# Adding 1e-6 to three of four attention denominators on ScalarE instead of TensorE, and moving their reciprocals

## The chip, the cores and the metric

The kernel runs on one core of one Trainium2 chip. A core has a matrix engine (TensorE, PE in the profile; its weight loads are listed apart as PEld), three engines for elementwise work (VectorE or DVE, ScalarE or ACT, GpSimd or POOL), SyncE (SP), whose queue issues most of the DMA transfers, an on-chip memory of 128 partitions (SBUF), and the accumulator memory PSUM that TensorE writes and VectorE and ScalarE read. The metric is the device time of the whole program in microseconds; lower is better.

## The reference, cut to what matters

The input x is 2048 tokens of 576 features in bfloat16. Four layers run in the order A, B, A, B, each on a layer norm of x and each added to x. A is linear attention with 32 heads of 18 features, B an MLP 576 -> 4608 -> 576 with a norm of its own in front. The same weights serve both A layers and both B layers.

```python
def _A_ref(x, wqkv, wo):
    q, k, v = qkv[0], qkv[1], qkv[2]            # of (x @ wqkv), 32 heads of 18
    phi = lambda t: jnp.where(t > 0, t + 1, jnp.exp(t)) + 1e-6
    pq, pk = phi(q), phi(k)
    kv = jnp.einsum("bhsd,bhse->bhde", pk, v)
    z = jnp.einsum("bhsd->bhd", pk)
    num = jnp.einsum("bhqd,bhde->bhqe", pq, kv)
    den = jnp.einsum("bhqd,bhd->bhq", pq, z)[..., None] + 1e-6
    o = num / den
    return (o, heads joined) @ wo

def _B_ref(x, w1, b1, w2, b2):
    y = _layernorm(x, axis=-1)
    h = _gelu(jnp.einsum("bsd,df->bsf", y, w1) + b1)
    return jnp.einsum("bsf,fd->bsd", h, w2) + b2

x = x + _A_ref(_layernorm(x, axis=-1), A_wqkv, A_wo)
x = x + _B_ref(_layernorm(x, axis=-1), B_w1, B_b1, B_w2, B_b2)
x = x + _A_ref(_layernorm(x, axis=-1), A_wqkv, A_wo)
x = x + _B_ref(_layernorm(x, axis=-1), B_w1, B_b1, B_w2, B_b2)
```

The change concerns `den`: the sum over a head's features of pq times z, plus 1e-6, and the reciprocal of it that scales the numerator.

## The kernel before, in words

All weights and x stay in SBUF. Tokens are worked on in 16 tiles of 128 and in 4 blocks of 512, numbered 0 to 3 in the code (the title of the change counts them 1 to 4). The order on every engine is the order in the source: the class InOrder (line 45) ties each instruction of VectorE (`vec`), ScalarE (`act`), GpSimd (`pool`) and SyncE (`sp`) to the one before it on that engine, and `pe` (line 217) does the same for TensorE. All matmuls go through `mm` (line 223), so they carry line 224 in the profile, and most work of the other engines carries line 53.

An A layer first walks the token tiles for keys and values, then forms the matrix of each head and multiplies it into `wo` (kv_wo). Query features pq of the four blocks are made by q_proj: TensorE projects, ScalarE evicts the result twice out of PSUM, as Exp and as Relu, and a later step `finish` on VectorE joins the two. Features are kept in five groups of up to seven heads (G = 5) with tokens along the free dimension, in slots of the tile `units`.

The denominators of a block come from den_stage (line 661). For each of five feature groups, four matmuls of 128 tokens each, in four column tiles of 32 rows, multiply pq with `zsel` (the sums of the keys, put in the columns of their heads); a sixth row of four multiplies `eps_sel`, filled with 1e-6, with the identity and so adds the 1e-6. VectorE takes the reciprocal out of PSUM into `rden`. For block 0 it is spread over the features by matmuls (scale_first). For blocks 1 to 3 it is written to DRAM (rden_rows), and `spread` (line 677) reads it back in seven transfers into `yT`, repeated for each feature of a head; scale_stage on VectorE then multiplies it into pq, and wo_stage multiplies the scaled pq with the head products and adds x (`residual`, on VectorE). wo_stage takes the bank pairs accA and accB of PSUM by turns, and so do the MLP groups.

The first MLP block is interleaved with the end of the A layer. After block 0's outputs come den_stage(1) and spread(1), a dummy Gelu that brings in the table of the Gelu (warm_table, line 782), the remaining `finish` steps, the scales of block 1, three MLP groups, den_stage(2) and (3), both spreads, the outputs of block 1, the scales of blocks 2 and 3, three more groups, the outputs of blocks 2 and 3, and two more groups. MLP groups are numbered here from 0.

An MLP group (m1_group, line 822) makes four tiles of 128 hidden features for 512 tokens. Its matmuls use half of the array's rows each, in pairs, and run in two halves of nine pairs. Between the halves, matmuls wait for a relay, a tiny copy on ScalarE (lines 864 and 865), that follows the end of other matmuls of the group. ScalarE evicts the four tiles with the Gelu and the bias b1: tiles 0 and 2 from a bank pair (hp_ps in the profile), tiles 1 and 3 from single banks (h_ps). Eviction 3 is held back until flush. Four single banks are used by turns for h_ps and den_ps.

Of the kernel before, what the change touches and what calls it, by code (L numbers as in the profile page):

```python
# [7 lines left out]
ACT = mybir.ActivationFunctionType  # L8
ALU = mybir.AluOpType
BF16 = mybir.dt.bfloat16  # L10
F32 = mybir.dt.float32
# [3 lines left out]
S, D, F, H, DH = 2048, 576, 4608, 32, 18  # L15
P = 128
# [4 lines left out]
G = 5  # L21
# [6 lines left out]
TPC = CB // P  # L28
CA = 512
# [6 lines left out]
def build(tc, A_x, A_wqkv, A_wo, B_w1, B_b1, B_w2, B_b2, out, n_layers=4):  # L36
    nc = tc.nc
    with ExitStack() as ctx:
        const = ctx.enter_context(tc.tile_pool(name="const", bufs=1))
# [52 lines left out]
        ident = const.tile([P, P], BF16, name="ident")  # L92
# [14 lines left out]
        quad_mask = const.tile([P, 4, P], BF16, name="quad_mask")  # L107
        zsel = const.tile([P, 6, H], BF16, name="zsel")
        eps_sel = const.tile([P, H], BF16, name="eps_sel")
        last_two = const.tile([P, 2], F32, name="last_two")  # L110
        zk = const.tile([P, P], BF16, name="zk")

        def mask_batches():
            sel, fill = pool.affine_select, pool.memset
            hb = head_bc[:, 0:4 * P].rearrange("p (g c) -> p g c", g=4)
            fours = head_bc[:, 4 * P:4 * P + 54].rearrange("p (h d) -> p h d", h=3)

            def maskz_a():
                first = fill(maskz[:], 1.0)
                sel(out=maskz[:], in_=maskz[:], compare_op=ALU.is_ge, fill=0.0,  # L120
                    base=0, pattern=[[-DH, 7], [0, DH]], channel_multiplier=1)
                sel(out=maskz[:], in_=maskz[:], compare_op=ALU.is_ge, fill=0.0,
                    base=DH - 1, pattern=[[DH, 7], [0, DH]], channel_multiplier=-1)
                return first

            def maskz_b():
                first = fill(zsel[:], 0.0)
                fill(eps_sel[:], 1e-6)
                fill(zk[:], 0.0)
                fill(last_two[:], 0.0)  # L130
                sel(out=last_two[:], in_=last_two[:], compare_op=ALU.not_equal, fill=1.0,
                    base=-126, pattern=[[-1, 2]], channel_multiplier=1)
                return first

            def heads_a():
                first = fill(head_sel[:], 1.0)
                part = head_sel[:, 0:5, :]
                sel(out=part, in_=part, compare_op=ALU.is_ge, fill=0.0,
                    base=0, pattern=[[126, 5], [-DH, H]], channel_multiplier=1)
                sel(out=part, in_=part, compare_op=ALU.is_ge, fill=0.0,  # L140
                    base=DH - 1, pattern=[[-126, 5], [DH, H]], channel_multiplier=-1)
                return first

            def heads_b():
                part = head_sel[:, 5, :]
                first = sel(out=part, in_=part, compare_op=ALU.is_ge, fill=0.0,
                            base=V4 - 64, pattern=[[-DH, H]], channel_multiplier=1)
                sel(out=part, in_=part, compare_op=ALU.is_ge, fill=0.0,
                    base=DH - 1 - (V4 - 64), pattern=[[DH, H]], channel_multiplier=-1)
                sel(out=part, in_=part, compare_op=ALU.is_ge, fill=0.0,  # L150
                    base=-64, pattern=[[0, H]], channel_multiplier=1)
                part = head_sel[:, 4, :]
                sel(out=part, in_=part, compare_op=ALU.is_ge, fill=0.0,
                    base=63, pattern=[[0, H]], channel_multiplier=-1)
                return first

            def quads_a():
                first = fill(quad_mask[:], 1.0)
                sel(out=quad_mask[:], in_=quad_mask[:], compare_op=ALU.is_ge, fill=0.0,
                    base=0, pattern=[[-32, 4], [0, P]], channel_multiplier=1)  # L160
                return first

            def quads_b():
                first = sel(out=quad_mask[:], in_=quad_mask[:], compare_op=ALU.is_ge, fill=0.0,
                            base=31, pattern=[[32, 4], [0, P]], channel_multiplier=-1)
                fill(head_bc[:], 0.0)
                return first

            def spread(quad):
                def ops():  # L170
                    first = sel(out=hb[:, :, 0:126].rearrange("p g (h d) -> p g h d", h=7),
                                in_=hb[:, :, 0:126].rearrange("p g (h d) -> p g h d", h=7), compare_op=ALU.not_equal, fill=1.0,
                                base=-32 * quad, pattern=[[-7, 4], [-1, 7], [0, DH]], channel_multiplier=1)
                    sel(out=fours, in_=fours, compare_op=ALU.not_equal, fill=1.0,
                        base=-32 * quad - 28, pattern=[[-1, 3], [0, DH]], channel_multiplier=1)
                    for part, n in ((hb[:, :, 126:128], [[0, 4], [0, 2]]), (head_bc[:, 4 * P + 54:4 * P + 64], [[0, 10]])):
                        sel(out=part, in_=part, compare_op=ALU.not_equal, fill=1.0,
                            base=-32 * quad - 31, pattern=n, channel_multiplier=1)
                    return first
                return ops  # L180

            return [maskz_a, maskz_b, heads_a, heads_b, quads_a, quads_b] + [spread(quad) for quad in range(4)]
# [40 lines left out]
        def mm(out_, lhsT, rhs, start, stop, **kw):  # L223
            return pe(nc.tensor.matmul(out_, lhsT=lhsT, rhs=rhs, start=start, stop=stop, **kw))  # L224
# [242 lines left out]
        def layer_A(li, next_kind, begin, before_tile, before_keys, mid_tile, rows_ahead, after_tile, q_tiles, placed, mlp):  # L467
# [192 lines left out]

            def den_stage(c):
                dp = one("den_ps", "one3" if c == 0 else None)
                for g in range(G + 1):
                    for j in range(TPC):
                        sel, by = (zsel[:, g + (g == 4 and c % 2), :], pq[(g, c)][:, j * P:(j + 1) * P]) if g < G else (eps_sel[:], ident[:])
                        mm(dp[32 * j:32 * (j + 1), 0:P], sel, by, g == 0, g == G)
                rden = work.tile([P, P], BF16, name="rden", bufs=2)
                with nc.allow_low_precision("reciprocal of the denominator in the reference's bfloat16"):
                    vec.reciprocal(out=rden[:], in_=dp[:, 0:P])
                if c > 0:  # L670

                    sp.dma_start(out=rden_rows[c].rearrange("h (j n) -> j h n", j=TPC), in_=rden[:])
                    return
                vec.tensor_tensor(out=quad_rden.rearrange("p (j n) -> p j n", j=4), in0=quad_mask[:],
                                  in1=rden[:].unsqueeze(1).to_broadcast([P, 4, P]), op=ALU.mult)

            def spread(c):
                heads, to = rden_rows[c], spare(c)
                at = 64 * (c % 2)
                for g in range(4):  # L680
                    sp.dma_start(out=to[0:126, g, :], in_=heads[7 * g:7 * g + 7, :].unsqueeze(1).to_broadcast([7, DH, CA]))
                sp.dma_start(out=to[126:P, 0:4, :], in_=heads[31:32, :].unsqueeze(1).to_broadcast([2, 4, CA]))
                sp.dma_start(out=to[at:at + 54, 4, :], in_=heads[28:31, :].unsqueeze(1).to_broadcast([3, DH, CA]))
                sp.dma_start(out=to[at + 54:at + 64, 4, :], in_=heads[31:32, :].to_broadcast([10, CA]))

            def scale_stage(g, c):
                rows = q_rows(g, c)
# [59 lines left out]
            q_next(True, "one0")  # L747
            finish(len(q_late) - 3)
            den_stage(0)
            kv_wo(0, act)  # L750
            kv_wo(1, act)
            q_next(True, "one1")
# [25 lines left out]
            q_next(True)  # L778
            first[3].transposed()
            den_stage(1)  # L780
            spread(1)
            warm_table(ACT.Gelu_apprx_tanh)
            assert not q_left
# [3 lines left out]
                for g in range(G):  # L787
                    scale_stage(g, c)

            def groups(n):  # L790
                for _ in range(n):
                    mlp.m1_group(0, mlp.done)
                    mlp.flush()

            def outputs(c):
                for t in range(c * TPC, (c + 1) * TPC):
                    wo_stage(t)

            finish(len(q_late))
            scales(1)  # L800
            groups(3)
            den_stage(2)
            den_stage(3)
            spread(2)
            spread(3)
            outputs(1)
            scales(2)
            scales(3)
            groups(3)
# [7 lines left out]
        class LayerB:  # L817
# [1 line left out]
                self.li, self.next_kind = li, next_kind  # L819
                self.hT, self.held, self.done = {}, None, 0  # L820

            def m1_group(self, c, g):
                hT = self.hT.setdefault(c, {})
                ctok = slice(c * CB, (c + 1) * CB)

# [32 lines left out]
                for i, (hi, n, wt, mv) in enumerate(order):  # L858
# [11 lines left out]
                    if n in (0, 2) and seen[0] == seen[2] == 9:  # L870
                        evict(0)
                        evict(2)
                    if n == 1 and seen[1] == 9:
                        evict(1)
                self.held = lambda: evict(3)
                self.done += 1

            def flush(self):
# [208 lines left out]
```

## Time and profile before

| | |
|---|---|
| median of 3 runs | 751.48 us (751.39 to 751.73) |
| the profiled execution | 751.55 us, its span 749.8 us |
| instructions | 15361 |
| TensorE matmuls | 745.2 us busy, 6437 |
| weight loads | 468.6 us, 6437 |
| VectorE | 269.1 us, 654 |
| ScalarE | 298.4 us, 652 |
| GpSimd | 114.9 us, 245 |
| den_ps matmuls of pq and zsel | 160, 219 ns each |
| den_ps matmuls of eps_sel | 32, 219 ns each |
| reciprocals | 8, 894 to 958 ns |

The busy rows say how much of the span each engine worked. The waits list who waited for whom, with the total, the number of times and the longest; the wait of a matmul mostly shows up at its weight load. In the timeline a row has the start and the duration in us, the engine, the line, the operation with what it writes and reads, and how many neighbours were merged into the row; a bracket holds the idle time of the engine before it and what ended it. Merged matmuls that run side by side overlap, so the starts of the rows say more than their durations.

### The profile page before, as it was taken

Reading aid. Unit: us, or ns where it says so; the run is one execution under the profiler, and the core shown is the slowest. Engines: PE = TensorE matmul, PEld = TensorE weight load, DVE = VectorE, ACT = ScalarE, POOL = GpSimd, SP = SyncE. Lnnn points to the kernel's source line nnn. Section 1 sums busy time; section 2 is a strip of 40 time slices with the busy share of each in tenths; the row PEclk is TensorE's granted clock in tenths of the full one; section 3 lists DMA queues with packets and bytes.
Section 4 is the critical chain, followed back from the end, with each engine's and each line's share of the span. In section 5 each row is a group of like instructions: output and inputs, shape, how many; then the busy total and the mean of one; then the engine's idle time right before and its main releaser. Section 6 shows DMA issues by size and latency. Waiting matters only on the chain.

```text
span 749.8 us, 15361 instructions
## 1 busy us (share of the span) xinstructions
PE 745.2 (99%) x6437; PEld 468.6 (63%) x6437; DVE 269.1 (36%) x654; ACT 298.4 (40%) x652; POOL 114.9 (15%) x245
## 2 busy tenths in 40 slices
PE   9999999999999999999999999999999999999998
PEld 5666455774576457646766665657646754774476
DVE  8987644334124303401365586432400140100000
ACT  5657743106601740374045474440274047205700
POOL 4541100322011201201200020022200120010010
PEclk9999999999999999999999999999999999999999
DMA  7991120022011202110032001102000200020000
GB/s 200 250 354 52 35 68 2 11 49 45 1 27 41 38 1 44 35 26 1 24 109 63 2 9 59 44 1 51 19 1 1 59 10 1 14 46 10 1 12 21
DMA packets 60381, 34.48 MB, mean 46 GB/s; under 512 B 36728, under 2 KB 60312, under 8 KB 60312
## 3 DMA queue, kind: packets, MB, share of 16 engines
q1 hardware_dynamic: 59560, 33.27, 17.4%
q8 instruction: 50, 0.82, 0.4%
q10 hardware_dynamic: 752, 0.23, 0.1%
q14 instruction: 19, 0.16, 0.1%
HBM read 21.70 MB, written 4.93 MB: 36 GB/s over the span
## 4 chain that ended last, share of the span: by engine, by line
PE 99%; DVE 0%; DMA 0%; issue 0%
PE m_ps L224 38%; PE hp_ps L224 21%; PE h_ps L224 17%; PE k_ps L224 6%; PE wo_ps L224 5%; PE q_ps L224 5%; PE rk_ps L224 4%; PE tp L383 1%; PE side_ps L224 1%; PE den_ps L224 0%; PE kvwo_ps L224 0%; PE kv_ps L224 0%; DMA x_sb<-in_A_x_dram 0%; PE rden_ps L224 0%; DVE ln_st L53 0%; PE side_tp L629 0%
## 5 line engine op out<-in xcount | busy, mean ns | idle before, releaser
L224 PEld LDWEIGHTS <-units 128*128 128x128 bf16 x2688 | 260.2, 98 | 74.5 <-issue 4.6
L224 PE MATMUL m_ps<-w_sb,units 128*128 128x288 bf16 (+2 forms) x2304 | 283.6, 286 | 0.0
L224 PEld LDWEIGHTS <-w_sb 64*128 64x128 bf16 x2304 | 123.9, 94 | 136.8 <-ACT relay_sb L53 4.1
L224 PE MATMUL h_ps<-yT,w_sb 64*128 64x512 bf16 x1152 | 178.0, 376 | 0.0
L224 PE MATMUL hp_ps<-yT,w_sb 64*128 64x512 bf16 x1152 | 148.0, 376 | 0.1
L53 DVE TENSOR_TENSOR x_sb<-m_ps,xo 128x576 bf16<-128x576 f32 (+2 forms) x33 | 24.4, 739 | 324.6 <-PE m_ps L224 324.6
L53 ACT COPY relay_sb<-relay_sb 128x1 f32<-128x1 f32 x144 | 27.7, 192 | 264.2 <-PE hp_ps L224 246.6
L53 ACT ACTIVATE units<-hp_ps,b1T 128x512 bf16<-128x512 f32 x144 | 91.2, 684 | 59.3 <-PE hp_ps L224 58.5
L53 POOL TENSOR_TENSOR xo<-x_sb,b_bc 128x576 f32<-128x576 bf16 x32 | 40.8, 1275 | 407.5 <-DVE x_sb L53 298.6
L53 ACT ACTIVATE units<-h_ps,b1T 128x512 bf16<-128x512 f32 x144 | 96.2, 688 | 0.0
L224 PE MATMUL hp_ps<-yT,w_tail 64*128 64x512 bf16 x144 | 54.1, 376 | 0.0
L224 PE MATMUL h_ps<-yT,w_tail 64*128 64x512 bf16 x144 | 54.1, 376 | 0.0
L224 PE MATMUL k_ps<-wkv_sb,yT 128*128 128x288 bf16 (+1 forms) x320 | 52.8, 302 | 0.0
L53 DVE BATCH_NORM_STATS2 ln_st<-x_sb 128x6 f32<-128x288 bf16 x128 | 51.3, 440 | 1.2 <-DMA x_sb<-in_A_x_dram 0.9
L53 ACT ACTIVATE phi_e<-k_ps 128x288 bf16<-128x288 f32 x64 | 26.4, 414 | 52.1 <-PE k_ps L224 50.7
L53 DVE STREAM_TRANSPOSE shared<-y_ring 128x640 bf16<-128x640 bf16 x40 | 32.9, 826 | 39.6 <-DMA yT<-shared 38.0
L53 ACT ACTIVATE units<-q_ps 128x512 bf16<-128x512 f32 x72 | 38.4, 596 | 21.4 <-PE q_ps L224 21.2
L53 DVE TENSOR_SCALAR y_ring<-x_sb,ln_mv,ln_rstd 128x576 bf16<-128x576 bf16 (+2 forms) x58 | 31.1, 538 | 40.7 <-POOL ln_rstd L53 40.5
L224 PE MATMUL q_ps<-yT,wq_sb 128*128 128x512 bf16 (+1 forms) x200 | 44.5, 380 | 0.0
L224 PE MATMUL wo_ps<-shared,units 128*128 128x288 bf16 x288 | 40.7, 286 | 0.0
L224 PEld LDWEIGHTS <-w_tail 64*128 64x128 bf16 x288 | 27.1, 94 | 17.0
L53 POOL TENSOR_TENSOR ln_rstd<-ln_u,neg_half 128x1 f32<-128x1 f32 x64 | 36.1, 564 | 8.5 <-DVE ln_u L53 3.5
(96 smaller groups left out, 421.1 us busy)
## 6 DMA issues: line engine op xcount, KB each, us to landing
yT<-shared SPq DMA_DIRECT2D x160, 40.0 KB
w_sb<-in_B_w_dram SPq DMA_DIRECT2D x12, 432.0 KB
w_sb<-in_B_w_dram SPq DMA_DIRECT2D x9, 512.0 KB
yT<-rden_rows SPq DMA_DIRECT2D x24, 126.0 KB
y_rows<-y_ring SPq DMA_DIRECT2D x16, 144.0 KB
units<-y_rows SPq DMA_DIRECT2D x16, 144.0 KB
x_sb<-in_A_x_dram SPq DMA_DIRECT2D x15, 144.0 KB
out_dram<-x_sb SPq DMA_DIRECT2D x15, 144.0 KB
```

Source lines behind the costliest of these rows:

```text
L53: inst = issue(*args, **kw)
L224: return pe(nc.tensor.matmul(out_, lhsT=lhsT, rhs=rhs, start=start, stop=stop, **kw))
L383: pe(nc.tensor.transpose(out=tp[:, k - a, :], in_=self.y[:, k * P:(k + 1) * P], identity=ident[:]))
```

## The change

Three things change, in both A layers alike.

First, den_stage issues the sixth row of matmuls only for block 0. For blocks 1 to 3 ScalarE adds the 1e-6: an activation Identity whose bias is a new column `den_eps` reads the bank of denominators in PSUM and writes it back in place. One GpSimd memset fills that column.

Second, the reciprocal and the write of its row become a function of their own. After block 1's den_stage it follows at once, as before. Those of blocks 2 and 3 come later: block 2's behind group 2 and both den_stages, then the first four transfers of spread(2), then three of block 1's four outputs, then block 3's reciprocal, the last three transfers of spread(2), spread(3), and the fourth output.

Third, in group 2 the evictions 1 and 3 are both held until den_stage(2) and (3), with their two Identities, are issued.

```diff
@@ maskz_b
                 fill(eps_sel[:], 1e-6)
+                fill(den_eps[:], 1e-6)
@@ den_stage
-                for g in range(G + 1):
+                for g in range(G):
                     for j in range(TPC):
-                        sel, by = (zsel[:, g + (g == 4 and c % 2), :], pq[(g, c)][:, j * P:(j + 1) * P]) if g < G else (eps_sel[:], ident[:])
-                        mm(dp[32 * j:32 * (j + 1), 0:P], sel, by, g == 0, g == G)
+                        mm(dp[32 * j:32 * (j + 1), 0:P], zsel[:, g + (g == 4 and c % 2), :], pq[(g, c)][:, j * P:(j + 1) * P],
+                           g == 0, g == G - 1 and c > 0)
+                if c == 0:
+                    for j in range(TPC):
+                        mm(dp[32 * j:32 * (j + 1), 0:P], eps_sel[:], ident[:], False, True)
+                else:
+                    act.activation(out=dp[:, 0:P], in_=dp[:, 0:P], func=ACT.Identity, bias=den_eps[:, 0:1], scale=1.0)
+                dens[c] = dp
+
+            def reciprocal(c):
                 rden = work.tile([P, P], BF16, name="rden", bufs=2)
-                    vec.reciprocal(out=rden[:], in_=dp[:, 0:P])
+                    vec.reciprocal(out=rden[:], in_=dens.pop(c)[:, 0:P])
                 if c > 0:
                     sp.dma_start(out=rden_rows[c].rearrange("h (j n) -> j h n", j=TPC), in_=rden[:])
@@ after block 0's outputs
             den_stage(1)
+            reciprocal(1)
             spread(1)
@@ groups
+            def groups(n, late=()):
+                for i in range(n):
+                    mlp.m1_group(0, mlp.done, bool(late) and i == n - 1)
+                    if i == n - 1:
+                        for step in late:
+                            step()
                     mlp.flush()
@@ the order
-            groups(3)
-            den_stage(2)
-            den_stage(3)
-            spread(2)
+            groups(3, [lambda: den_stage(2), lambda: den_stage(3)])
+            reciprocal(2)
+            spread(2, slice(0, 4))
+            outputs(1, slice(0, 3))
+            reciprocal(3)
+            spread(2, slice(4, 7))
             spread(3)
-            outputs(1)
+            outputs(1, slice(3, TPC))
             scales(2)
             scales(3)
@@ m1_group
-                    if n == 1 and seen[1] == 9:
+                    if n == 1 and seen[1] == 9 and not hold:
                         evict(1)
-                self.held = lambda: evict(3)
+                self.held = lambda: [evict(n) for n in ((1, 3) if hold else (3,))]
```

More of the change, by code (lines that the diff above doesn't have):

```diff
@@ L109, in build @@
         eps_sel = const.tile([P, H], BF16, name="eps_sel")
+        den_eps = const.tile([P, 1], F32, name="den_eps")
         last_two = const.tile([P, 2], F32, name="last_two")
@@ L662, in den_stage @@
                 dp = one("den_ps", "one3" if c == 0 else None)
-                for g in range(G + 1):
+                for g in range(G):
                     for j in range(TPC):
-                        sel, by = (zsel[:, g + (g == 4 and c % 2), :], pq[(g, c)][:, j * P:(j + 1) * P]) if g < G else (eps_sel[:], ident[:])
-                        mm(dp[32 * j:32 * (j + 1), 0:P], sel, by, g == 0, g == G)
+                        mm(dp[32 * j:32 * (j + 1), 0:P], zsel[:, g + (g == 4 and c % 2), :], pq[(g, c)][:, j * P:(j + 1) * P],
[6 more added lines that the diff above has]
+                dens[c] = dp
+            dens = {}
+            def reciprocal(c):
                 rden = work.tile([P, P], BF16, name="rden", bufs=2)
                 with nc.allow_low_precision("reciprocal of the denominator in the reference's bfloat16"):
-                    vec.reciprocal(out=rden[:], in_=dp[:, 0:P])
+                    vec.reciprocal(out=rden[:], in_=dens.pop(c)[:, 0:P])
                 if c > 0:
@@ L675, in den_stage, with spread @@
                                   in1=rden[:].unsqueeze(1).to_broadcast([P, 4, P]), op=ALU.mult)
-            def spread(c):
+            def spread(c, part=slice(0, 7)):
                 heads, to = rden_rows[c], spare(c)
                 at = 64 * (c % 2)
[L680 to L684, printed above, removed]
+                moves = [(to[0:126, g, :], heads[7 * g:7 * g + 7, :].unsqueeze(1).to_broadcast([7, DH, CA])) for g in range(4)] + \
+                        [(to[126:P, 0:4, :], heads[31:32, :].unsqueeze(1).to_broadcast([2, 4, CA])),
+                         (to[at:at + 54, 4, :], heads[28:31, :].unsqueeze(1).to_broadcast([3, DH, CA])),
+                         (to[at + 54:at + 64, 4, :], heads[31:32, :].to_broadcast([10, CA]))]
+                for dst, src in moves[part]:
+                    sp.dma_start(out=dst, in_=src)
             def scale_stage(g, c):
@@ L749, in layer_A @@
             den_stage(0)
+            reciprocal(0)
             kv_wo(0, act)
@@ L788, in scales, with outputs @@
                     scale_stage(g, c)
-            def groups(n):
-                for _ in range(n):
-                    mlp.m1_group(0, mlp.done)
+            def groups(n, late=()):
[4 more added lines that the diff above has]
+                            step()
                     mlp.flush()
-            def outputs(c):
-                for t in range(c * TPC, (c + 1) * TPC):
+            def outputs(c, part=slice(0, TPC)):
+                for t in range(c * TPC, (c + 1) * TPC)[part]:
                     wo_stage(t)
@@ L820, in __init__, with m1_group @@
                 self.hT, self.held, self.done = {}, None, 0
-            def m1_group(self, c, g):
+            def m1_group(self, c, g, hold=False):
                 hT = self.hT.setdefault(c, {})
```

## The prediction

> **What bounds the kernel now.** I read the page's busy rows first, then the waits of TensorE's weight loads, then the timeline around the edited places.
>
> ```profile
> PE 745.2 (99%) x6437; PEld 468.6 (63%) x6437; DVE 269.1 (36%) x654; ACT 298.4 (40%) x652; POOL 114.9 (15%) x245
> PEclk9999999999999999999999999999999999999999
> ```
>
> TensorE is busy for 745.2 of 749.8 us at the full granted clock. A microsecond taken out of TensorE's queue is a microsecond gained; work on ScalarE, VectorE, POOL or SP costs nothing until TensorE has to wait for it. Where it already waits, the waits of the weight loads tell (total, times, longest):
>
> ```profile
> PEld L224 <- issue: 12.9, 40, 0.4
> PEld L224 <- ACT relay_sb L53: 4.1, 14, 0.4
> ```
>
> Those on ACT are the relays, the tiny ScalarE copies of m1_group between the two halves of a group. Most only take up the weight load's lead. One per A layer is different. Layer 0 at den_stage(1) in the timeline (start, duration):
>
> ```profile
> 78.68 3.01 ACT L53 ACTIVATE units<-q_ps 128x512 bf16<-128x512 f32 x6
> ...
> 80.77 0.46 PE L224 MATMUL den_ps<-units,zsel 128*32 128x128 bf16 x20
> 80.77 0.49 DVE L53 COPY yT<-tp 128x640 bf16<-128x640 bf16 x1 [0.33 <-PE tp L383]
> ...
> 81.05 0.24 PE L224 MATMUL den_ps<-ident,eps_sel 128*32 128x128 bf16 x4
> ...
> 81.32 1.04 PE L224 MATMUL hp_ps<-yT,w_sb 64*128 64x512 bf16 x8
> 81.34 0.96 DVE L53 RECIPROCAL rden<-den_ps 128x128 bf16<-128x128 f32 x1
> 81.71 1.28 ACT L53 ACT_TABLE_LOAD   x1
> ...
> 83.12 0.17 ACT L53 COPY relay_sb<-relay_sb 128x1 f32<-128x1 f32 x1
> ...
> 83.34 0.54 PEld L224 LDWEIGHTS <-w_sb 64*128 64x128 bf16 x8 [0.40 <-ACT relay_sb L53]
> 83.35 1.04 PE L224 MATMUL hp_ps<-yT,w_sb 64*128 64x512 bf16 x8
> ```
>
> ScalarE is packed from 78.68 to the relay's end at 83.29: six evictions, the table load, the 0.20 us dummy Gelu at 83.01, the relay. The relay's TensorE half starts 0.06 us later. A half-group undisturbed takes 1.94 us (85.30 to 87.24), so TensorE would have been ready at 81.32 + 1.94 = 83.26 and already loses 0.09 us. The second A layer has the same picture: group at 448.88, table load at 449.27, relay at 450.68, second half at 450.91, again 2.03 us. These are the only two places where ScalarE sets TensorE's pace around the edit. The other two denominators:
>
> ```profile
> 93.16 0.46 PE L224 MATMUL den_ps<-units,zsel 128*32 128x128 bf16 x20
> ...
> 93.45 0.23 PE L224 MATMUL den_ps<-ident,eps_sel 128*32 128x128 bf16 x4
> ...
> 93.51 0.45 PE L224 MATMUL den_ps<-units,zsel 128*32 128x128 bf16 x20
> 93.56 1.27 ACT L53 ACTIVATE units<-h_ps,b1T 128x512 bf16<-128x512 f32 x2
> ...
> 93.73 1.77 DVE L53 RECIPROCAL rden<-den_ps 128x128 bf16<-128x128 f32 x2 [1.34 <-PE den_ps L224]
> ...
> 93.95 0.67 PE L224 MATMUL wo_ps<-shared,units 128*128 128x288 bf16 x4
> ```
>
> **Matmuls removed.** Each matmul lasts 0.22 us, but four column tiles run side by side: one denominator's 24 take 0.35 us of the queue (93.16 to 93.51), 0.058 us per row of four, and the eps row is 93.45 to 93.51. Stages 2 and 3 are followed by TensorE's own work, so both rows come out whole: 2 x 0.058 = 0.117 us per layer, 0.23 in two. Stage 1 gives nothing: the MLP group behind it starts at 81.32, 0.06 after VectorE's copy of yT ends (80.77 + 0.49 = 81.26), and that copy is untouched. Bounds for all six rows: 0 and 0.35.
>
> **Identity at den_stage(1).** It lands in the packed stretch, between the last eviction of q and the table load, on the chain relay to TensorE. The trace has no ScalarE write into PSUM. Nearest row: the Gelu with a bias column out of PSUM, 128x512, 686 ns. Columns cost 0.81 ns each (the 512-column q eviction of 596 against the 288-column exponential of 414), so 128 columns are 686 - 384 x 0.81 = 375 ns. Neighbours overlap: six q evictions take 3.01 us, a pitch of 483 for 596, so 113 ns are hidden, and the table load moves by 0.26 us. Lower end: the 128x72 cast out of PSUM, 213 ns, plus 56 columns, less the overlap, 0.15. Upper end: the 128x576 Identity of the layer norms, 868 ns, less 448 columns, without overlap, 0.51. I take 0.26, the Gelu being nearest in form. Less than nothing is excluded: an added instruction can't shorten a queue without a gap. TensorE is already late behind this relay, so all of it arrives there: +0.26 per layer, +0.52 in two. ScalarE has its next gap at 84.63 (0.91 idle), so the delay does not go on there; TensorE cannot make it up.
>
> Behind the same Identity stands VectorE: reciprocal 1 starts at about 82.0, not 81.34, 0.66 later, and with it the nine late finishes (82.21 to 88.83), the write of rden_rows, SP's spread(1) (84.47, seven issues) and the five scales of block 1 (90.51 to 92.40, then to 93.06). Stage 2 needs the finishes at 93.16, the output products need the scales at 93.95: covered by 3.7 and 0.9 us. Without that cover it would be up to 0.66 a layer.
>
> **Identities 2 and 3, held evictions.** In group 2 evictions 1 and 3 now wait for two Identities. Evictions 0 and 2 end at 93.67, when stage 2's matmuls finish, so the Identities take about 93.7 to 94.35 and the evictions end near 95.5, not 94.83. Their banks are wanted by group 3 at 98.95 and ScalarE's next work is at 100.30: nothing. Reciprocal 2 moves from 93.73 to about 94.15 and ends near 95.1; block 1's first residual is next on VectorE, ready at about 95.4 when its products are done (it began at 95.53 behind both reciprocals). TensorE wants that bank back at 96.41. Nothing, with 0.2 us in hand; a reciprocal later by more than that would stall the third output tile.
>
> **Reciprocal 3 and SP's order.** Reciprocal 3 goes behind the third residual (97.83 + 0.76 = 98.59) and takes about 0.9, so the fourth residual starts near 99.5 rather than 99.06. Its bank pair is next used by group 4 at 102.85: nothing. SP issues rden_rows of block 2 near 95.1, four spreads from about 97.3, then stands waiting until reciprocal 3 ends at 99.5. Behind that wait are the write of block 3's row, three spreads of block 2 and seven of block 3. At 10.72 us for fourteen, 0.77 each, the last issue of block 2 ends near 102.4 and of block 3 near 107.7, against 107.60 now. Scales 2 slip from 103.18 to about 104.2, scales 3 stay near 109.2; outputs want them at 110.72 and, four tiles of 1.23 later, 115.6. Cover above 4 us.
>
> **POOL.** One memset of 128x1, 0.10 us by neg_half's row, in a batch followed by 1.35 us of idle POOL: nothing.
>
> **Sum.** -0.23 + 0.52 = +0.29 us. On the profiled execution's 751.55 that is 751.84; the median of the three runs is 0.07 lower, so I say 751.8. With the ends of the Identity: +0.06 to +0.79; with no matmul time saved either, +1.02.
>
> **Rivals.** *The stall is not passed on* (faster, unmeasurably): if the Identity ran inside other work of ScalarE, only the matmuls would count, -0.23, or -0.35 if stage 1's row counted too: 751.1 to 751.25. Against it stands the packed row from 78.68 to 83.29.
>
> *A table reload* (slower): if Identity is not among the functions loaded with the Gelu, Identity 2 would be preceded by a 1.28 us table load and the held evictions by another. The second falls into ScalarE's 5.47 us of idle before 100.30. The first moves Identity 2 to 95.0, reciprocal 2 to about 95.45 to 96.4, the first residual's end to 97.15; the third output tile, due at 96.41, starts 0.8 late, 1.6 in two layers: 751.48 + 0.29 + 1.6 = 753.4. It decides from 0.2 us of delay on. For it: no Identity runs after the Gelu load in this trace. Against it: before that load Exp, Relu, Copy and Identity share one table, Copy runs under the Gelu's, and the page counts four loads in all. The Trainium skill's "ScalarE: Activation LUTs", section "Table sets: the hidden batching unit", says that cheap functions, identity among them, are in every set; by it this rival cannot happen, and no run here shows it for Identity under Gelu. The same page, section "What ACT_TABLE_LOAD costs", adds a drain of about 1.38 us to each load; the trace disagrees, since the load of 81.71 takes 1.28 and the dummy Gelu starts at 83.01, right behind it. With the drain the reload would cost about 2.8 more in two layers, near 756.2.
>
> *SP's wait reaches the scales* (slower): the last rows of block 2 sit behind reciprocal 3. It decides once they land over 4 us later than I work out; 1 us beyond, twice, gives 753.8. SP's other issues show no such delay.
>
> **How the numbers follow.** Small loss as summed 0.74; stall hidden 0.17; reload 0.04; SP's wait 0.03; faster in a way that I can't name 0.02. About 0.2%, 1.5 us, is what a measurement of this kernel tells from no change; the first two lie within it: same 0.91, slower 0.07, faster 0.02. Range 751.1 to 752.5: from all matmul time saved and no stall, to the dearest Identity with nothing saved. It leaves out about 1 in 10.
>
> **What would show it.** In the changed profile: 24 fewer TensorE matmuls, eps_sel only in den_stage(0). An Identity of about 0.37 us between the last eviction of q and the table load; the second half of group 0 starting about 2.3 us after the first, not 2.03. The two later stages 0.29 us apart, not 0.35. Four table loads. Residuals of block 1 still 1.23 us apart, the last about 0.4 late. I am wrong if the first-half pitch stays 2.03, if a table load stands near stage 2, or if output tiles or group 3 start after a gap.

## The result, and the profile after

The changed kernel takes 753.54 us (median of 9 runs, 752.92 to 755.57); the kernel before, run beside it, 751.63 us (9 runs, 751.39 to 751.79). The ratio is 1.0027, with a 95% interval of 1.0017 to 1.0038: slower by 1.9 us, where +0.3 was forecast and 752.5 was the upper end. A second set on another occasion gave 753.12 against 751.34, ratio 1.0023 (1.0014 to 1.0033). The ratios weigh all executions, so they need not equal the quotient of two medians. One execution of this study, of the kernel with the Identity twice below, took 4481.83 us and is left out of its figures.

Most of the small things went as worked out; one thing that was written off as covered did not. First the waits of the weight loads after (total, times, longest):

```profile
PEld L226 <- ACT relay_sb L53: 4.6, 14, 0.6
...
PEld L226 <- DVE units L53: 1.8, 3, 1.2
```

And the waits of the matmuls themselves, in which before had only that of the warm-up:

```profile
PE wo_ps L226 <- DVE units L53: 0.9, 1, 0.9
```

The relays went from 4.1 to 4.6, the longest from 0.4 to 0.6. New is an output matmul that waits for VectorE's scaling of `units`. (The second list also has 0.4 us of transposes, tp, and 0.3 us of the first projection, k_ps, all within the first 10 us.)

Following the starts of the same matmuls in both profiles, TensorE falls behind as follows. It is 0.44 us late once the start-up is over, 0.23 more at the relay of layer 0, then gains 0.11 at den_stage 2 and 3, loses 1.11 at the outputs of blocks 2 and 3 of layer 0, 0.24 at the second layer's relay, gains 0.11 there, and loses 0.04 at its outputs. The sum, 1.84, is the difference of the spans (751.6 against 749.8). The 0.44 is not put down to the change: over the profiles of this study the first projection starts anywhere between 6.4 and 6.9 us, and the same changed kernel started it at 6.93 in this profile and at 6.63 in its second. What sets that start was not followed further. In the second profile of the same changed kernel the start-up is 0.06 earlier than before's, the outputs lose 0.71 in layer 0 and 0.38 in layer 2, and the span is 751.1.

Layer 0 around den_stage(1), timeline of the changed kernel:

```profile
81.75 1.04 PE L226 MATMUL hp_ps<-yT,w_sb 64*128 64x512 bf16 x8
81.98 0.38 ACT L53 ACTIVATE den_ps<-den_ps,den_eps 128x128 f32<-128x128 f32 x1
82.38 1.28 ACT L53 ACT_TABLE_LOAD   x1
82.39 0.96 DVE L53 RECIPROCAL rden<-den_ps 128x128 bf16<-128x128 f32 x1 [0.69 <-ACT den_ps L53]
...
83.78 0.40 ACT L53 COPY relay_sb<-relay_sb 128x1 f32<-128x1 f32 x2
84.01 0.54 PEld L226 LDWEIGHTS <-w_sb 64*128 64x128 bf16 x8 [0.63 <-ACT relay_sb L53]
84.01 1.04 PE L226 MATMUL hp_ps<-yT,w_sb 64*128 64x512 bf16 x8
```

The Identity stands between the evictions of q and the table load, the relay follows later, and the first half of MLP group 0 takes 84.01 - 81.75 = 2.26 us instead of 2.03. That is the stall that was forecast.

The place that decided lies 27 us later. First the kernel before, timeline of layer 0, SP's transfers and what waits for them (not shown so far):

```profile
94.72 1.36 SPq L53 DMA_DIRECT2D rden_rows<-rden  x2
96.88 10.72 SPq L53 DMA_DIRECT2D yT<-rden_rows  x14
```

```profile
109.17 1.89 DVE L53 TENSOR_TENSOR units<-yT,units 128x512 bf16<-128x512 bf16 x5 [4.24 <-DMA yT<-rden_rows]
...
110.72 2.50 PE L224 MATMUL wo_ps<-shared,units 128*128 128x288 bf16 x19
```

Then the changed kernel:

```profile
93.83 0.74 PE L226 MATMUL den_ps<-units,zsel 128*32 128x128 bf16 x40
94.34 0.62 ACT L53 ACTIVATE den_ps<-den_ps,den_eps 128x128 f32<-128x128 f32 x2
...
94.72 0.96 DVE L53 RECIPROCAL rden<-den_ps 128x128 bf16<-128x128 f32 x1 [0.75 <-ACT den_ps L53]
...
95.70 0.57 SPq L53 DMA_DIRECT2D rden_rows<-rden  x1
...
97.84 3.71 SPq L53 DMA_DIRECT2D yT<-rden_rows  x4
...
99.06 0.95 DVE L53 RECIPROCAL rden<-den_ps 128x128 bf16<-128x128 f32 x1
...
101.64 0.57 SPq L53 DMA_DIRECT2D rden_rows<-rden  x1
102.26 7.45 SPq L53 DMA_DIRECT2D yT<-rden_rows  x10
...
110.93 1.89 DVE L53 TENSOR_TENSOR units<-yT,units 128x512 bf16<-128x512 bf16 x5 [4.44 <-DMA yT<-rden_rows]
111.27 0.66 PE L226 MATMUL wo_ps<-shared,units 128*128 128x288 bf16 x4
...
112.87 2.38 PE L226 MATMUL wo_ps<-shared,units 128*128 128x288 bf16 x18 [0.93 <-DVE units L53]
```

The reader is to see three things. SP's last transfer is issued by 109.71 instead of 107.60. The scales of block 3 end at 112.82 instead of 111.06. And block 2's first output tile, begun at 111.27, stops after four matmuls until exactly then: its fifth starts at 112.87. Before, that fifth matmul started at 111.22 with the last scale done at 111.06, hardly more than the 0.05 us that TensorE takes to follow VectorE. What looked like an undisturbed stretch had about 0.1 us of cover. In the second A layer, layer 2, the same scale of the kernel before ends at 477.74 and is wanted at 478.78, some 1.0 us of cover, and there the loss is only 0.04.

Why block 2's outputs need a scale of block 3: group 4, three heads and ten of the eighteen features of a fourth, fills only 64 of the 128 rows, so `q_proj` puts group 4 of two blocks into one slot of `units` (`pq[(g, c + i)] = dst`). The output matmul of block 2 reads all 128 rows of it, with zero weights for the other half; the program's dependencies make it wait for whoever writes that slot.

### The profile page after: what moved, and what is told of

It reads as the page before. It is cut to its first block, busy times and chain, and to the rows that moved or that the text cites. A ratio compares the mean times of both kernels' runs of the same rounds, so it can differ in the third digit from the quotient of the medians.

```text
span 751.6 us, 15303 instructions
## 1 busy us (share of the span) xinstructions
PE 745.2 (99%) x6413; PEld 468.1 (62%) x6413; DVE 269.0 (36%) x654; ACT 300.2 (40%) x658; POOL 114.9 (15%) x246
## 4 chain that ended last, share of the span: by engine, by line
PE 94%; ACT 2%; DVE 2%; DMA 1%; POOL 1%; issue 1%; SPq 0%; DVEq 0%
PE m_ps L226 38%; PE hp_ps L226 20%; PE h_ps L226 16%; PE k_ps L226 6%; PE wo_ps L226 4%; PE q_ps L226 4%; PE rk_ps L226 4%; ACT units L53 1%; PE side_ps L226 1%; DVE units L53 1%; DMA x_sb<-in_A_x_dram 1%; PE tp L385 1%; ACT y_ring L53 0%; SPq L53 0%; DVE ln_st L53 0%
```

## The experiments

Three theories were set against each other. A: the shared slot, fed late by SP's new order. B: the new tile den_eps shifts what lies behind it in memory and slows the transfers. C: the Identities ahead of the reciprocals cost all of it. Each set of runs had runs of the kernel before beside it, and "against" gives the median of these. Code cuts show edited lines only, against the changed kernel unless said otherwise; "group 0" is the first MLP group, whose first half the Identity at den_stage(1) lengthened.

**The new order alone**, with all 1e-6 by matmuls:

```diff
+            groups(3)
+            den_stage(2)
+            den_stage(3)      # with the matmuls of eps_sel, no Identity, no held eviction
             reciprocal(2)
             spread(2, slice(0, 4))
             outputs(1, slice(0, 3))
             reciprocal(3)
```

> The kernel before with the new places of the reciprocals and transfers only; the 1e-6 stays with the matmuls, no Identity, no held evictions. Theory A (shared slot): the query features of group 4 of blocks 2 and 3 lie in one slot, so block 2's first output waits for the last scale of block 3, which in the profile before ends at 111.06, 0.1 us ahead of its use; the new order of SP's transfers makes that scale late. Then the outputs of block 2 in layer 0 wait 0.5 to 1 us here too, the first half of MLP group 0 keeps its 2.03 us, and the time is 0.5 to 1.0 us above before, 752.1 to 752.6. Theory B (memory): the new tile den_eps shifts the tiles behind it in memory and makes the transfers slower; it is absent here, so the time is that of before, 751.6 within 0.3. Theory C (ScalarE): all of the loss comes from the Identities ahead of the reciprocals; 751.6 here too.

Measured 751.88 us (11 runs) against 751.45, ratio 1.0006 (0.9997 to 1.0015). The first half of group 0 is back at 2.03 us. TensorE loses 0.73 us at block 2's outputs in layer 0 and nothing in layer 2. Waits of the matmuls:

```profile
PE wo_ps L224 <- DVE units L53: 0.6, 1, 0.6
```

The time alone, 0.43 above, lies below the range that A gave and would fit B and C. The profiled execution took 752.55 us, one of the three longest of the 11, so most of them are likely to have waited less than it did. What speaks for A is the wait in the profile: it comes without den_eps and without any Identity.

**The Identities alone**, with the reciprocals and transfers in the old order:

```diff
             reciprocal(2)
+            reciprocal(3)
+            spread(2)
+            spread(3)
+            outputs(1)
-            spread(2, slice(0, 4))
-            outputs(1, slice(0, 3))
-            reciprocal(3)
-            spread(2, slice(4, 7))
-            spread(3)
-            outputs(1, slice(3, TPC))
```

> The changed kernel with both reciprocals ahead of block 1's outputs and the transfers in the order of before; the Identities, the held evictions and den_eps stay. Theory A: the first half of MLP group 0 takes about 2.26 us in both layers (+0.23 each), the two rows of matmuls give back 0.11 each, and the wait at block 2's outputs in layer 0 shrinks to 0.2 to 0.5 us, what the later reciprocals still cost: 752.0 to 752.5, about half of the loss gone. Theory B: the slow transfers stay, 753 or more. Theory C: the whole loss stays, 753.5.

Measured 752.25 (11 runs) against 751.45, ratio 1.0011 (1.0002 to 1.0020). The time is in the range that A gave, but by luck: no wait is left at block 2's outputs, so that part of the expectation missed, and in its place comes another wait. The whole loss of theory C is not there either. Timeline of this kernel, block 1's residuals:

```profile
94.06 1.77 DVE L53 RECIPROCAL rden<-den_ps 128x128 bf16<-128x128 f32 x2 [1.55 <-ACT den_ps L53]
...
95.86 1.42 DVE L53 TENSOR_TENSOR x_sb<-wo_ps,x_sb 128x576 bf16<-128x576 f32 x2
...
96.67 0.65 PE L226 MATMUL wo_ps<-shared,units 128*128 128x288 bf16 x4 [0.20 <-DVE x_sb L53]
```

Both reciprocals start 0.33 later than in the profile before (93.73), behind the Identities, the first residual ends late, and the third output tile waits for its bank. Counted by the starts of the matmuls it costs 0.36 us in each layer, more than the 0.11 of the saved rows. So the two halves of the change hang together: without the new place of reciprocal 3 the Identities stall block 1's outputs, and with it SP is late for block 2's.

**Group 4 of block 3 first**, in the transfers and in the scales:

```diff
             def scales(c):
-                for g in range(G):
+                for g in (range(G) if c < 3 else (4, 0, 1, 2, 3)):
                     scale_stage(g, c)
@@ spread
+                if c == 3:
+                    moves = moves[5:] + moves[:5]
                 for dst, src in moves[part]:
```

> The changed kernel, but of block 3 the transfers of group 4 are issued first and its scale of group 4 is the first of the five. Theory A: block 2's outputs no longer wait (before: 0.93 at the matmul and 1.2 at the weight load in layer 0), the rest of block 3's scales being wanted 4.9 us later; 1 us or more of the 1.9 goes, 751.9 to 752.5, and the runs lie closer together than the 752.9 to 755.6 of the changed kernel. Theories B and C: the same transfers and the same Identities, so only a part of the wait goes; 753 or more.

Measured 752.03 (11 runs, 751.59 to 752.43) against 751.45, ratio 1.0007 (0.9998 to 1.0015). The wait is gone, and so is the scatter of the changed kernel's runs. Timeline of this kernel:

```profile
106.94 0.42 DVE L53 TENSOR_TENSOR units<-yT,units 64x512 bf16<-64x512 bf16 x1 [1.19 <-DMA yT<-rden_rows]
110.80 5.44 PE L226 MATMUL wo_ps<-shared,units 128*128 128x288 bf16 x43
110.83 1.43 DVE L53 TENSOR_TENSOR units<-yT,units 128x512 bf16<-128x512 bf16 x4 [3.47 <-DMA yT<-rden_rows]
112.24 0.76 DVE L53 TENSOR_TENSOR x_sb<-wo_ps,x_sb 128x576 bf16<-128x576 f32 x1
```

The scale of the shared slot ends at 107.4, and block 2's tiles run straight through while the other four scales of block 3 are still going until 112.26. This is the test that separates A from B and C: same tile in memory, same Identities, only the order of equal work differs. In this profile TensorE's delay is 0.24 over both layers, made of +0.23 and -0.11 in each, as the prediction had it without the transfers. The profiled execution, at 751.73, is one of the faster of the 11, and the median lies 0.58 above before; the interval does not tell 0.24 from 0.58, and a second link, found further below, may make up the difference.

**den_eps at the end of the memory:**

```diff
-        den_eps = const.tile([P, 1], F32, name="den_eps")     # behind eps_sel
+        den_eps = const.tile([P, 1], F32, name="den_eps")     # behind act_dummy, the last constant
```

> The changed kernel with den_eps allocated behind all other constants, so that every other tile lies where it lay before. Theory A: nothing changes, 753.2 to 753.9. Theory B: transfers land as before, the first projection starts at 6.5 and not at 6.9 us, the wait at block 2's outputs goes, and the time falls to about 752.0.

Measured 752.77 (11 runs, 752.47 to 754.78) against 751.45, ratio 1.0023 (1.0014 to 1.0032). The ratio is that of the changed kernel's second set; the median is below the range that A gave, 1.32 above before where the changed kernel had 1.78 and 1.91. The wait stays, and TensorE loses 0.80 at the outputs in layer 0:

```profile
PE wo_ps L226 <- DVE units L53: 0.6, 1, 0.6
```

B falls as the cause of the wait. The first projection starts at 6.58 here, but at 6.63 in the second profile of the changed kernel too, so the place of den_eps does not set it. Whether that place is worth a few tenths of a microsecond these runs do not tell.

**The changed kernel again**, for comparison with those that follow:

> The changed kernel as it is, so that the others can be compared with it on one chip. Its wait at block 2's outputs in layer 0 depends on when SP's transfers land: 0.7 to 1.2 us; relay half of group 0 2.26 us in both layers; 752.7 to 753.7.

Measured 753.12 (9 runs) against 751.34, as told above. The first half of group 0 takes 2.26 us in both layers.

**Block 1 by matmuls again**, on top of group 4 first:

```diff
-                           g == 0, g == G - 1 and c > 0)
-                if c == 0:
+                           g == 0, g == G - 1 and c > 1)
+                if c <= 1:
                     for j in range(TPC):
                         mm(dp[32 * j:32 * (j + 1), 0:P], eps_sel[:], ident[:], False, True)
```

> The changed kernel with block 3's group 4 first in the transfers and the scales, and block 1's 1e-6 added by matmuls again. If the Identity ahead of the table load is what lengthens the first half of MLP group 0, that half is back at 2.03 us in both layers, and the four rows of matmuls of blocks 2 and 3 are all that is left of the change: 0.23 us below before, 751.2 to 751.5. Theory C (the Identities of blocks 2 and 3 cost by themselves): still 0.2 to 0.5 above before.

Measured 751.49 (11 runs) against 751.34, ratio 1.0000 (0.9991 to 1.0009). The first half of group 0 is back at 2.03 us in both layers: the Identity ahead of the table load is what lengthened it. But the 0.23 did not show. The profiled execution, at 751.98 the longest of the 11, says where it can go:

```profile
110.51 2.62 PE L226 MATMUL wo_ps<-shared,units 128*128 128x288 bf16 x20
111.60 1.43 DVE L53 TENSOR_TENSOR units<-yT,units 128x512 bf16<-128x512 bf16 x4 [4.12 <-DMA yT<-rden_rows]
112.95 1.41 DVE L53 TENSOR_TENSOR x_sb<-wo_ps,x_sb 128x576 bf16<-128x576 f32 x2
113.76 2.49 PE L226 MATMUL wo_ps<-shared,units 128*128 128x288 bf16 x19 [0.63 <-DVE x_sb L53]
```

A second link stood behind the first. Block 3's other scales, late from the transfers, are in front of block 2's residuals on VectorE, and the third output tile waits for the first residual's bank; TensorE loses 0.79 there in layer 0 and nothing in layer 2. The expectation of the run with group 4 first, that those scales are wanted only 4.9 us later, overlooked this queue.

**Group 4 first in the kernel before**, the same two edits on the old kernel:

> The kernel before with block 3's group 4 first in the transfers and the scales, nothing else. Theory A: before has only 0.1 us of cover there, so nothing is gained in most executions, within 0.1 of before; the cover for the group 4 scale grows from 0.1 to some 4 us.

Measured 751.39 (11 runs) against 751.34, ratio 1.0001 (0.9992 to 1.0010). As expected, before does not gain. The scale of group 4 did get its cover: it ends at 106.29 and is wanted at 111.32, 5 us later. But by the second link the other four scales of block 3 have only some 0.6 us. They end at 111.84, 0.42 before the first residual's matmuls do, and the residual ends at 113.02, 0.26 before its bank is wanted at 113.28, of which 0.05 goes to the hand-over.

**The Identity twice**, for block 1, on top of group 4 first:

```diff
                     act.activation(out=dp[:, 0:P], in_=dp[:, 0:P], func=ACT.Identity, bias=den_eps[:, 0:1], scale=1.0)
+                    if c == 1:
+                        act.activation(out=dp[:, 0:P], in_=dp[:, 0:P], func=ACT.Identity, bias=den_eps[:, 0:1], scale=1.0)
```

> The changed kernel with block 3's group 4 first, and block 1's Identity issued twice, so that its denominators get 2e-6. If the Identity delays the relay one for one, the first half of MLP group 0 goes from 2.26 to 2.5 us in both layers (one more Identity of 0.38 less some 0.1 of overlap each), and the time is 0.5 to 0.6 us above the kernel with one Identity. If TensorE had slack there, nothing changes.

Measured 753.23 (median of 10) against 751.34, ratio 1.0023 (1.0014 to 1.0032). Timeline:

```profile
81.55 0.75 ACT L53 ACTIVATE den_ps<-den_ps,den_eps 128x128 f32<-128x128 f32 x2
82.32 1.28 ACT L53 ACT_TABLE_LOAD   x1
...
83.95 1.04 PE L226 MATMUL hp_ps<-yT,w_sb 64*128 64x512 bf16 x8 [0.52 <-ACT relay_sb L53]
```

The first half of group 0 goes from 2.26 to 2.63 us in both layers. The second Identity costs its whole 0.37, where 0.24 was expected: it reads what the first writes, and the two don't overlap. ScalarE's time before the relay reaches TensorE one for one. The time lies 1.9 above before, more than expected; the rest of the loss is the second link again, 0.57 and 0.39 us. That part is not shown to come from the second Identity. Against the run with group 4 first, SP's first transfer of block 2 in layer 0 is 0.42 later and TensorE at the outputs 0.41, so the two kept step; but SP's last ten transfers take 7.34 us instead of 6.82, all of it in a longer wait before block 3's first transfer, which the profile puts down to block 3's row.

**Denominators one group earlier**, with the Identities for blocks 2 and 3, block 1 by matmuls:

```diff
-            scales(1)
-            groups(3, [lambda: den_stage(2), lambda: den_stage(3)])
+            groups(2, [lambda: den_stage(2), lambda: den_stage(3)])
             reciprocal(2)
-            spread(2, slice(0, 4))
-            outputs(1, slice(0, 3))
             reciprocal(3)
-            spread(2, slice(4, 7))
+            spread(2)
             spread(3)
-            outputs(1, slice(3, TPC))
+            scales(1)
+            groups(1)
+            outputs(1)
```

> Block 1's 1e-6 by matmuls as before; den_stage 2 and 3, with their Identities and held evictions, behind MLP group 1 instead of group 2, both reciprocals and all transfers right behind, then block 1's scales and group 2. The transfers of blocks 2 and 3 start some 3.5 us earlier, so the theory of the shared slot and of the residuals behind VectorE's scales has no wait left in either layer, and the reciprocals are no longer ahead of block 1's residuals. Only the four rows of matmuls remain: 0.23 below before, 751.1 to 751.4, with a rival that block 1's scales, now behind two reciprocals, come late for block 1's outputs: then 0.2 to 0.6 above before.

Measured 753.08 (11 runs) against 751.45, ratio 1.0022 (1.0013 to 1.0031). Both the hope and its rival missed. Block 1's scales are in time; the wait sits in group 2:

```profile
90.27 1.26 ACT L53 ACTIVATE units<-h_ps,b1T 128x512 bf16<-128x512 f32 x2
```

```profile
91.58 1.04 PE L226 MATMUL h_ps<-yT,w_sb 64*128 64x512 bf16 x8 [0.45 <-ACT units L53]
```

The evictions held back for the Identities end at 91.53 and keep banks that group 2 wants at once: it takes 4.80 us (89.89 to 94.69) where it took 3.98 in the kernel before (89.18 to 93.16), and TensorE is 0.8 us later in each layer, with the saved matmuls already taken off. In the changed kernel four output tiles stand between the held evictions and the next group, which is why holding cost nothing there.

**The same order by matmuls alone:**

> The same order with all 1e-6 by matmuls, as before: what the order alone does. Nothing in the profile of before waits there, so within 0.15 of before, and some 0.2 above the same order with the Identities.

Measured 751.69 (11 runs) against 751.45, ratio 1.0004 (0.9996 to 1.0013). That is 0.24 above before, just outside the 0.15 expected. Its profile starts 0.23 late; by the matmuls' starts it loses 0.15 more in each layer where it meets the moved denominators. So most of the 1.6 us is not the order's; it comes with the Identities and the evictions held behind them, for which TensorE is seen to wait.

**Block 3's other scales behind block 2's residuals**, with group 4 first and block 1 by matmuls:

```diff
-            scales(3)
+            scales(3, slice(0, 1))      # group 4
             groups(3)
-            outputs(2)
+            outputs(2, slice(0, 1))
+            scales(3, slice(1, 3))
+            outputs(2, slice(1, 2))
+            scales(3, slice(3, 5))
+            outputs(2, slice(2, 4))
```

> The kernel with block 3's group 4 first and block 1's 1e-6 by matmuls, with the other four scales of block 3 moved behind the residuals of block 2's first and second tile, two each. In the run without this move TensorE waited 0.6 us at block 2's third tile in layer 0, for a residual queued on VectorE behind scales whose transfers were late. If that queue is the cause, this wait falls to 0.3 us or less; if it is the transfers themselves, the wait moves to block 3's first tile and stays 0.6 or more. Time 751.2 to 751.6.

Measured 751.16 (11 runs) against 751.45, ratio 0.9998 (0.9989 to 1.0007). No output matmul waits:

```profile
110.48 5.57 PE L226 MATMUL wo_ps<-shared,units 128*128 128x288 bf16 x44
111.92 0.76 DVE L53 TENSOR_TENSOR x_sb<-wo_ps,x_sb 128x576 bf16<-128x576 f32 x1 [3.71 <-PE wo_ps L226]
112.59 0.75 DVE L53 TENSOR_TENSOR units<-yT,units 128x512 bf16<-128x512 bf16 x2
113.26 0.75 DVE L53 TENSOR_TENSOR x_sb<-wo_ps,x_sb 128x576 bf16<-128x576 f32 x1
```

The first residual no longer stands behind late scales, so the queue on VectorE was the second link. Identities 2 and 3 are in place here and cost nothing, so theory C falls for them. TensorE's only lasting differences from before are two steps of -0.11 us. The same kernel once more:

> The last kernel once more, beside a new set of runs of the kernel before. Its only lasting difference on TensorE is four rows of matmuls, 0.23 us: a median 0.1 to 0.4 below before. If the 0.29 of the first time was scatter, the medians agree within 0.1.

Measured 751.09 (11 runs) against 751.44, ratio 0.9995 (0.9986 to 1.0004). The medians lie 0.29 and 0.35 below and the profile accounts for 0.23, but the interval includes no change both times: the gain that the four rows of matmuls hold is there in the starts of the matmuls and too small to be shown by these times.

## Why the prediction was wrong

**The relay was right.** Forecast +0.26 us per layer for the Identity at den_stage(1); measured 2.26 against 2.03, +0.23 in both layers, gone without that Identity, and more with two. The Identity lasted 0.38 us where 0.375 was worked out from the Gelu's row, and the table load moved by 0.23.

**The matmuls were right.** Two rows of four for 0.117 per layer: measured 0.11 in every profile with the Identities in these places. Stage 1's row gave nothing, as group 0 waits for the copy of yT.

**Identities 2 and 3 and the held evictions were right for this kernel.** No wait at block 1's outputs, none at group 3. The caution that a reciprocal later by more than 0.2 us would stall the third output tile is what the run with the Identities alone showed, at 0.36 a layer.

**The step that failed is "Reciprocal 3 and SP's order".** It said of blocks 2 and 3: "outputs want them at 110.72 and, four tiles of 1.23 later, 115.6. Cover above 4 us." Block 3's scale of group 4 was wanted at 111.22 in layer 0, for the slot that both blocks share, and had 0.1 us. Its other scales are wanted by about 112.4: block 2's first residual, 0.76 long, queues behind them on VectorE and has to free the bank of the third output tile, which starts at 113.18. They end at 111.06 and had 1.3 us. Neither shows as a wait in the profile before, since both were met. They show in the code, in q_proj's two names for one slot and in the order `scales(3)`, `outputs(2)`.

The same step also had SP too early: block 3's last issue "near 107.7", measured 109.71. The 2.11 against before come in four parts in layer 0. Reciprocal 2 brings 0.96: 0.67 is TensorE's own delay by then, which moves the outputs as well, and 0.3 the Identity. The first four transfers gain 0.06. The write of block 3's row brings 0.66, because it now stands between the spreads, where before it used the time in which SP waits for block 2's row to land. The last ten transfers bring 0.55, mostly one gap of 0.59 before block 3's first transfer. The profile puts 0.5 of that gap down to SP waiting for block 3's row to land: between 92 and 112 us its waits for such rows are two, 2.0 us together, and were one of 0.7 before. SP never stood waiting for reciprocal 3, as the prediction had it: that was done at 100.01 and SP was issuing until 101.55. By the prediction's own 0.77 a transfer, four of them from 97.3 end at 100.4, not before 99.5; with the write at 0.57 and ten more transfers the last issue is at 108.65, not 107.7.

**The rivals.** SP's wait reaching the scales was named, and given 0.03 with a decision point of over 4 us; the point was 0.1 us in layer 0. What happened is its kind of chain, late transfers to late scales to waiting outputs, but by block 3's scales and without the wait for reciprocal 3. The sign that the prediction set for itself, an output tile that starts after a gap, is in the profile. With the right cover but the last issue at 107.7, 0.1 later than before, the working would have stayed near +0.29. With the issue at 108.65, 1.05 later, it would have been some 0.95 more in layer 0 and next to nothing in layer 2, whose cover was 1.0: about +1.2, still below the 1.9 measured. The table reload did not happen: four table loads in all, and the Identities behind the Gelu's load ran at once (the first starts 0.01 us behind the Gelu eviction in front of it), as the Trainium skill's "ScalarE: Activation LUTs", section "Table sets: the hidden batching unit", has it.

## What to carry to other kernels

A stretch without waits tells nothing of how much cover it has: before moving a transfer, measure for each consumer the time between the end of the work that releases it and its start, and take the consumers from the code, with every slot that two of them share and every instruction queued behind the late one. When transfers are reordered, count those that were issued into a gap of the queue, because they cost their whole issue time once the gap is elsewhere, and see whether the wait for their landing is still covered. Removing matmuls from a full TensorE was worth their place in its queue, here 0.06 us for four side by side, and not the 0.22 that each row shows. The engine that takes the work over needs idle time at that place: the Identity of block 1 stood on ScalarE ahead of a relay that TensorE was already waiting for and cost 0.23, those of blocks 2 and 3 cost nothing once the transfers behind them were in order.

## What the runs showed of the hardware that was not expected

An Identity of 128x128 from PSUM into the same place in PSUM with a bias column takes 342 ns, and 380 at den_stage(1), where it starts 0.15 us before the activation in front of it ends; none of the rows before had ScalarE write into PSUM. The Trainium skill's "ScalarE: Activation LUTs", section "What ACT_TABLE_LOAD costs", gives about 280 ns plus 0.833 per column with such a bias, an estimate of 387 for 128 columns; the rows lie a little below it. Two of them in place, one reading the other's result, take 0.75 us together; two on different banks, 0.62.

The kernels with the wait at block 2's outputs scatter more: the changed kernel's 9 runs span 752.9 to 755.6 and 752.8 to 754.4, the 11 with den_eps moved 752.5 to 754.8, those with group 4 first 751.6 to 752.4. The kernel before spans 751.4 to 751.8 in its first set; of the 31 and 33 in two later sets one each stands at 753.1 and the others are below 752. The output loss was 1.11 and 0.04 us in the two layers of one profile, 0.71 and 0.38 in the other. That the landing of the transfers makes this scatter is likely and not shown, since only one execution of each set is profiled.
